# Attention with exchanged halves for the odd heads: products of both column halves beside each other, scores in quarters of the array

## The chip, the cores and the metric

The kernel runs on one core of a Trainium2 chip, as one program. The metric is the device time of one execution in microseconds; a kernel's time is the median of its runs. The core has five engines that matter here: PE (TensorE, matrix products, with a weight load recorded as PEld), DVE (VectorE), ACT (ScalarE), POOL (GpSimd) and SP (SyncE, which issues the DMAs). Each engine takes its instructions in order.

## The reference

Three parts follow one another, all in fp32. First a linear attention with a state, over 4 batches x 8 heads = 32 heads, 768 steps, 40 channels:

```python
for t in range(S):
    y[:, :, t] = np.einsum('bhd,bhde->bhe', rt, state)
    Sa = np.einsum('bhde,bhe->bhd', state, at)
    state_decay = state * wt[:, :, None, :] - np.einsum('bhd,bhe->bhde', Sa, bt)
    state = state_decay + np.einsum('bhd,bhe->bhde', vt, kt)
```

Then y, as 3072 tokens of 320 numbers, goes through a first expert, max(0.01 h, h) of h = x @ w_in (320 x 2048), times w_out, and through a second, sigmoid(x @ w_gate) * (x @ w_val) (1536 hidden), times w_out2.

## The kernel before, in words

**Chunks.** The 768 steps are cut into 12 chunks k of C = 64 steps; two make a block n (NB = 6), ci is the chunk in its block. The 32 heads are four groups q of eight. A group's eight heads are pairs: i = 0..3 counts pairs, h = 0, 1 the even and the odd head of a pair. Head h lies on partitions 64h to 64h+39 (D = 40 channels, the rest zeros).

**Preparation of a group (n, q).** `load` (L116) brings w, a and kb. In a the two heads of a pair stand block-diagonally, with zeros between them, so that one matmul of 128 x 128 gives both. `decays` (L138) runs cumulative products of w on DVE (L145, L151). `scale` (L156) multiplies a (L162) and kb (L165) by them, once per chunk; for block 0 part of this is on POOL, as the list `DVE0` says. `products` (L169) makes the scores sc of a against k and b, one matmul per chunk and pair (L177 to L179), one PSUM bank per chunk, and copies them out: ACT into Ld (L183) and Lo (L189), then the masked part against k into X, on DVE (L198), or on ACT and POOL for block 1 (L192, L195). `turned` (L202) transposes a (L209) and copies it into columns 64 to 103 of X (two copies a chunk, L214, one for each half of the partitions), then transposes kb (L217) into G (L220). `ranges` (L222) tests w.

**Solve.** `inverse` (L237) inverts the 32 x 32 triangles of all heads of a block, on POOL (on DVE for block 0). `solved` (L265) puts the inverse of 64 steps together with small products m (L279, L286) and multiplies it with X: the products qp (L294), copied to QT (L296).

**Recurrence.** `recur` (L315) takes one chunk of one group. It loads r into R (L326), v into W (L332) and, in `load_state` (L299), v transposed into FL (L303). The state is copied into W below v (L334). FL holds for each pair 64 columns of v transposed and 64 of the state transposed; the products fp of FL and R (L339) are masked into W (L341). The products pm of QT and W (L347) follow, one bank for each h, always on output partitions 64 to 127 (column half 64 to 128 of the array); ACT (L350) and DVE (L352) put them back into W. The products yp (L359, L362, L365) give the output y (L381) and the next state S (L369), which is transposed (L374) into FL of the next chunk (L376). In yp the heads alternate between output partitions 0 to 63 and 64 to 127.

**Order.** The order of the work is written out at the end of `attention` (L404 to L461): for each block n, groups in pairs; `together` (L395) runs the chunk of two groups in turns, four steps of the next block's inverse before each turn; the preparation of block n+2 stands around them. The program is built with a planner that simulates the engines and fixes each engine's order by it, so instructions of several stages mix. All DMAs are issued by SP, in order. The experts (class at L472, L598 on) come after; their weights are decoded by ACT, DVE and POOL when the attention ends.

**Layout.** `_layout` lays out the inputs on the host, outside the time.

Of the kernel before, what the change touches and what calls it, by code (L numbers as in the profile page):

```python
# [23 lines left out]
NQ, NX, NT = 10, 16, 2  # L24
HP = G // 2
C = 64
# [5 lines left out]
XF = 2 * C  # L32


def attention(ctx, tc, A, xT, bad, prods):
# [12 lines left out]
    masks = const.tile([128, 3, C], FP32, name="masks")  # L48
# [6 lines left out]
    TTx, G2x, Los, Gs, As, Rs, FLs, STs = [], [], [], [], [], [], [], []  # L55
    for i in range(2):
        Los.append(eb.tile([128, G, 32], FP32, bufs=1, name=f"Lo{i}"))
    for i in range(NX):
        Gs.append(two.tile([128, 8 * D + 24], FP32, bufs=1, name=f"G{i}"))
    for i in range(2):  # L60
        TTx.append(eb.tile([128, 8, 128], FP32, bufs=1, name=f"TTx{i}"))
        G2x.append(eb.tile([128, 8, 2, 32], FP32, bufs=1, name=f"G2x{i}"))
        As.append(ea.tile([128, 4, 2, 2, C], FP32, bufs=1, name=f"a{i}"))
# [8 lines left out]
    for i in range(6):  # L72
        STs.append(two.tile([128, 4, C], FP32, bufs=1, name=f"S{i}"))
        FLs.append(two.tile([128, 4, XF], FP32, bufs=1, name=f"FL{i}"))
# [13 lines left out]
    def zeros():  # L88

        for t in [t[:, 8 * D:] for t in Gs] + TTx + G2x + Rs + STs + [t[:, :, C:XF] for t in FLs] + Los[1:]:  # L90
            nc.gpsimd.memset(t, 0.0)
# [24 lines left out]
    def load(n, q):  # L116

        if q == 0:
            st["L", n] = (ea.tile([128, G, 32], FP32, tag="Ld", bufs=1, name="Ld"),
                          Los[n % 2])  # L120
        load_w(n, q)
        if n == 0 and q > 1:
            a = eb.tile([128, 4, 2, 2, C], FP32, tag="TTc", bufs=NT, name="a")
# [12 lines left out]
        st["in", n, q] = a, kb  # L136
# [31 lines left out]

    def products(n, q):  # L169


        a, kb = st["in", n, q]
        Ld, Lo = st["L", n]
        for ci in range(2):
            g0 = 8 * q + 4 * ci
            sc = bank(n, "sc")
            for i in range(4):  # L177
                nc.tensor.matmul(  # L178
                    out=sc[:, i].rearrange("p a s -> p (a s)"), lhsT=a[:, i, ci].rearrange("p a s -> p (a s)"),  # L179
                    rhs=kb[:, i, ci].rearrange("p a s -> p (a s)"), start=True, stop=True)  # L180
            for r in range(4):
                x, c0 = slice(32 * r, 32 * r + 32), 32 * (r % 2)
                nc.scalar.copy(out=Ld[x, g0:g0 + 4], in_=sc[x, :, 1, c0:c0 + 32])  # L183
# [3 lines left out]
            for r in (1, 3):  # L187
                x = slice(32 * r, 32 * r + 32)
                st["Lo", n, q] = nc.scalar.copy(out=Lo[x, g0:g0 + 4], in_=sc[x, :, 1, 0:32])  # L189
            X = eb.tile([128, 4, X1], FP32, tag="X", bufs=NX, name="X")  # L190
            if n == 1:
                nc.scalar.copy(out=X[:, :, 0:C], in_=sc[:, :, 0])  # L192
                for half in range(2):
                    x = X[64 * half:64 * half + 64, :, 0:C]
                    nc.gpsimd.affine_select(out=x, in_=x, pattern=[[0, 4], [-1, C]], base=0, channel_multiplier=1,  # L195
                                            compare_op=ALU.is_gt, fill=0.0)
            else:
                nc.vector.tensor_tensor(out=X[:, :, 0:C], in0=sc[:, :, 0], in1=bc(masks[:, 0], 4), op=ALU.mult)  # L198
            st["X", n, q, ci] = X
            st["G", n, q, ci] = Gs[(8 * n + 2 * q + ci) % NX]  # L200

    def turned(n, q):  # L202

        a, kb = st["in", n, q]
        for ci in range(2):
            X, g = st["X", n, q, ci], st["G", n, q, ci]
            tr = bank(n, "tr")
# [57 lines left out]
    def solved(n, q):  # L265
# [21 lines left out]
        for half in range(2):  # L287
            x = slice(64 * half, 64 * half + 32)
            nc.scalar.copy(out=tt[x, :, 64 * half + 32:64 * half + 64], in_=m2[0:32, :, half])
        for ci in range(2):  # L290
            X = st.pop(("X", n, q, ci))
# [4 lines left out]
            nc.scalar.copy(out=qt[0:X1].rearrange("p i h s -> p i (h s)"), in_=qp[0:X1])  # L296
            st["QT", n, q, ci] = qt

    def load_state(k, q):  # L299
# [3 lines left out]
        nc.sync.dma_start(out=FL[:, :, 0:C], in_=A["vT"][:, k, q])  # L303
# [8 lines left out]
    def by8(x):  # L312
        return x.rearrange("p e (u x) -> p e u x", x=8)

    def recur(n, q, ci):  # L315
# [12 lines left out]
        W = two.tile([128, X1 // 8, 8, 8], FP32, tag="W", bufs=3, name="W")  # L328
        we = W.rearrange("p u e x -> p e u x")
        Wv, Wf = we[:, :, 0:D // 8], we[:, :, D // 8:]  # L330
# [12 lines left out]
        cols, u0 = slice(0 if more else D, X1), 0 if more else D // 8  # L343
        for h in range(2):
            pm, e = bank2(n, "pm", [128, 4, 128]), slice(4 * h, 4 * h + 4)
            for i in range(4):
                nc.tensor.matmul(out=pm[C:2 * C, i, cols], lhsT=QT[0:X1, i, h], rhs=W[0:X1, u0:, 4 * h + i],  # L347
                                 start=True, stop=True)
            if more:
                st["Hs", n, q, ci] = nc.scalar.activation(out=Wv[C:2 * C, e], in_=by8(pm[C:2 * C, :, 0:D]),  # L350
                                                          func=AF.Copy, scale=-1.0)
            nc.vector.tensor_tensor(out=Wf[C:2 * C, e], in0=by8(pm[C:2 * C, :, D:X1]),  # L352
                                    in1=by8(bc(masks[C:2 * C, 2], 4)), op=ALU.mult)
# [3 lines left out]
        for j in range(2):  # L357
            for h in range(2):
                nc.tensor.matmul(out=yp[64 * h:64 * h + 64, 2 * j:2 * j + 2, D:X1], lhsT=FL[:, 2 * h + j, C:XF],  # L359
# [3 lines left out]
        for h, i, e in heads:  # L363
            g0 = D * (2 * i + h)
            nc.tensor.matmul(out=yp[64 * h:64 * h + 64, i, cols], lhsT=Gt[:, g0:g0 + 64], rhs=W[:, u0:, e],  # L365
                             start=False, stop=i == 3)
        if more:
# [8 lines left out]
            nc.scalar.copy(out=FL1[:, :, C:X1].rearrange("p (h j) d -> p j h d", h=2),  # L376
                           in_=st_.rearrange("p j (h d) -> p j h d", h=2)[:, :, :, 0:D])
# [443 lines left out]
def _layout(inputs):  # L821
# [16 lines left out]
    A["a"] = heads(a).reshape(2, D, NB, 2, 4, 4, C).transpose(0, 1, 2, 4, 5, 3, 6).reshape(2, D, NB, 4, 8, C)  # L838
    pairs = (2, 6, 4, 0, 3, 1, 5)
    A["r"] = r.reshape(B, 2, 2, 2, NC, C, D).transpose(pairs).reshape(2, D, NC, 4, 4, C)  # L840
    A["kb"] = np.stack([em(k), em(b)], 2).reshape(128, 4, 4, 2, NB, 2, C).transpose(0, 4, 1, 2, 5, 3, 6)
    vT = np.zeros((2, 64, NC, 4, 4, C), f)
    vT[:, :D] = v.reshape(B, 2, 2, 2, NC, C, D).transpose(pairs).reshape(2, D, NC, 4, 4, C)
    A["vT"] = vT.reshape(128, NC, 4, 4, C)
    A["v"] = v.reshape(B, 4, 2, NC, C, D // 8, 8).transpose(4, 3, 0, 5, 2, 1, 6).reshape(C, NC, 4, D // 8, 8, 8)
# [6 lines left out]
    m = np.zeros((128, 3, C), f)  # L852
    m[:, 0] = np.tile(low, (2, 1))
    m[:C, 1] = low.T
    m[C:X1, 1] = 1
    m[C:, 2] = -low.T
# [29 lines left out]
```

## Time and profile before

| | us |
|---|---|
| median of 3 runs (1284.63 to 1288.41) | 1285.53 |
| the profiled execution: its own time | 1287.13 |
| its span, first to last instruction | 1285.4 |
| PE busy in the span | 1173.8 |
| DVE, ACT, POOL busy | 749.9, 620.5, 328.3 |

Granted TensorE clock, mean over the span: 0.968 of full speed. The attention ends with the last y at 523 us; the experts take the rest.

How to read it: a row of the groups gives line, engine, operation, output<-inputs by the names in the program, shapes, count, then the busy time in us, the mean of one in ns, and the idle time of the engine just before such instructions with what ended it. A chain row is a piece of the path that ended last. Ends of matmuls are modelled, so two matmuls are compared by their starts; a few records of matmuls can be missing. Every fp32 matmul is recorded as two.

### The profile page before, as it was taken

What the parts mean: (1) busy time and instruction counts of PE and PEld (TensorE: products, weight loads), DVE (VectorE), ACT (ScalarE), POOL (GpSimd) and SP (SyncE); (2) the same over time, 40 slices, a digit from 0 to 9 for tenths busy, and PEclk for the clock granted to TensorE, in tenths of its full rate; (3) what the DMA queues carried; (4) which work ended last, traced back from release to release, by engine and by line L of the source; (5) the groups of instructions that cost most, each with busy time, mean ns of one, the idle gap of its engine ahead of it and who ended that gap; (6) DMA issues with size and microseconds to landing.
All of it is one profiled execution on the core that took longest, in us unless ns stands there. A gap on an engine that the chain in (4) does not pass through costs nothing.

```text
span 1285.4 us, 21419 instructions
## 1 busy us (share of the span) xinstructions
PE 1173.8 (91%) x7954; PEld 1006.9 (78%) x7954; DVE 749.9 (58%) x1455; ACT 620.5 (48%) x1510; POOL 328.3 (26%) x498
## 2 busy tenths in 40 slices
PE   4629988999889998899999999998999999999997
PEld 4528777888778887678778888887888888888886
DVE  9993766656663434899985444489972323222222
ACT  4737746667556453567664433356552323222221
POOL 9338373561726300244420000022320000000000
PEclk8769989999899999999999999999999999999999
DMA  6413224333231222433441010025320100000000
GB/s 192 126 44 88 76 64 106 108 85 83 57 84 48 66 67 68 120 101 103 117 121 40 21 46 26 21 81 151 105 80 1 46 1 21 1 21 1 21 1 24
DMA packets 105394, 84.54 MB, mean 66 GB/s; under 512 B 46656, under 2 KB 90432, under 8 KB 105280
## 3 DMA queue, kind: packets, MB, share of 16 engines
q1 hardware_dynamic: 105280, 83.07, 23.3%
q8 instruction: 65, 1.06, 0.3%
q14 instruction: 49, 0.40, 0.1%
HBM read 71.25 MB, written 11.80 MB: 65 GB/s over the span
## 4 chain that ended last, share of the span: by engine, by line
PE 66%; DVE 17%; ACT 8%; issue 4%; DMA 4%; POOL 1%; SPq 0%; DVEq 0%; ACTq 0%; POOLq 0%
PE h L579 18%; PE o L579 9%; PE o L595 9%; PE pm L347 5%; PE o L689 3%; PE o L690 3%; PE o L691 3%; PE qp L294 3%; ACT Ld L183 2%; PE fp L339 2%; DVE c L145 2%; PE yp L365 2%; DVE a L162 2%; PE m L279 1%; PE sc L178 1%
## 5 line engine op out<-in xcount | busy, mean ns | idle before, releaser
L579 PE MATMUL h<-xh,up 128*128 128x512 f32 x624 | 201.2, 394 | 8.5 <-DVE g L587 7.6
L579 PE MATMUL h<-xl,up 128*128 128x512 f32 x624 | 194.6, 392 | 0.0
L569 ACT CAST gh<-g 128x512 fp32r<-128x512 f32 x168 | 104.0, 620 | 176.8 <-DVE g L702 118.3
L570 DVE TENSOR_TENSOR gl<-g,gh 128x512 fp32r<-128x512 f32 x168 | 122.5, 730 | 72.3 <-ACT gh L569 72.2
L702 DVE TENSOR_TENSOR g<-o,t 128x512 f32<-128x512 f32 x72 | 49.6, 690 | 190.6 <-PE o L579 190.2
L579 PEld LDWEIGHTS h<-xh,up 128*128 128x128 f32 x624 | 116.7, 188 | 36.0 <-DVE g L587 10.3
L579 PEld LDWEIGHTS h<-xl,up 128*128 128x128 f32 x624 | 117.5, 189 | 22.8
L595 PE MATMUL o<-gh,down 128*128 128x512 f32 x450 | 132.0, 390 | 1.0 <-ACT gh L569 1.0
L698 ACT ACTIVATE t<-h 128x512 f32<-128x512 f32 x72 | 42.9, 596 | 126.5 <-PE h L579 126.4
L595 PEld LDWEIGHTS o<-gh,down 128*128 128x128 f32 x450 | 84.5, 188 | 19.4 <-ACT gh L569 1.8
L587 DVE TENSOR_TENSOR g<-h,t 128x512 f32<-128x512 f32 x96 | 65.8, 686 | 55.6 <-ACT t L586 55.2
L250 POOL TENSOR_TENSOR tmp<-T 128x30 f32<-128x30 f32 (+9 forms) x150 | 86.7, 578 | 42.1 <-DVE T L243 28.8
L511 POOL TENSOR_TENSOR down<-f,e 128x256 fp32r<-128x256 f32 (+2 forms) x41 | 39.7, 983 | 225.9 <-PE o L595 171.4
L347 PE MATMUL pm<-W,QT 104*64 104x104 f32 (+1 forms) x768 | 80.9, 261 | 14.9 <-DVE W L341 14.2
L595 PE MATMUL o<-gl,down 128*128 128x512 f32 x270 | 90.4, 389 | 0.0
L579 PE MATMUL o<-xh,up 128*128 128x512 f32 x288 | 89.2, 390 | 0.5 <-POOL up L511 0.5
L255 POOL TENSOR_TENSOR T<-T,tmp 128x30 f32<-128x30 f32 (+9 forms) x150 | 86.4, 576 | 11.1
L579 PE MATMUL o<-xl,up 128*128 128x512 f32 x288 | 88.5, 389 | 0.0
L347 PEld LDWEIGHTS pm<-W,QT 104*64 104x64 f32 x768 | 71.1, 142 | 20.7 <-DVE W L341 15.3
L586 ACT ACTIVATE t<-h 128x512 f32<-128x512 f32 x96 | 56.7, 592 | 61.1 <-PE h L579 61.0
L689 PE MATMUL o<-down,gh 128*128 128x320 f32 x264 | 80.1, 309 | 0.4 <-ACT gh L569 0.4
L690 PE MATMUL o<-down,gh 128*128 128x320 f32 x264 | 80.3, 308 | 0.0
(267 smaller groups left out, 2337.4 us busy)
## 6 DMA issues: line engine op xcount, KB each, us to landing
kb<-in_kb SPq DMA_DIRECT2D x24, 512.0 KB
rd<-in_w_out SPq DMA_DIRECT2D x28, 320.0 KB
w<-in_w SPq DMA_DIRECT2D x24, 260.5 KB
FL<-in_vT SPq DMA_DIRECT2D x48, 128.0 KB
ru<-in_w_in SPq DMA_DIRECT2D x16, 384.0 KB
ru<-in_w_gate SPq DMA_DIRECT2D x12, 384.0 KB
ru<-in_w_val SPq DMA_DIRECT2D x12, 384.0 KB
a<-in_a SPq DMA_DIRECT2D x48, 80.0 KB
```

The lines of the kernel that those rows point to most:

```text
L250: eng.tensor_tensor(out=tv, in0=T[:, i0:i1, j:j + 1].to_broadcast([128, i1 - i0, j]), in1=T[:, j:j + 1, 0:j].to_broadcast([128, i1 - i0, j ...
L255: steps.append(eng.tensor_tensor(out=T[:, i0:i1, 0:j], in0=T[:, i0:i1, 0:j], in1=tv, op=ALU.add))
L347: nc.tensor.matmul(out=pm[C:2 * C, i, cols], lhsT=QT[0:X1, i, h], rhs=W[0:X1, u0:, 4 * h + i], start=True, stop=True)
L569: copy = self.nc.scalar.copy(out=gh, in_=g)
L570: self.last = copy.ins, (engine or self.nc.vector).tensor_tensor(out=gl, in0=g, in1=gh, op=ALU.subtract).ins
L579: self.nc.tensor.matmul(out=ps, lhsT=l, rhs=r, start=(i == 0), stop=(i == len(ops) - 1))
L586: self.nc.scalar.activation(out=t, in_=h, func=AF.Copy, scale=0.01)
L587: self.nc.vector.tensor_tensor(out=g, in0=h, in1=t, op=ALU.max)
L595: self.nc.tensor.matmul(out=acc, lhsT=l, rhs=r, start=first and i == 0, stop=last and i == len(ops) - 1)
L689: nc.tensor.matmul(out=o, lhsT=gj, rhs=w[:, 0], start=s, stop=False)
L690: nc.tensor.matmul(out=o, lhsT=gj, rhs=w[:, 1], start=False, stop=False)
L702: nc.vector.tensor_tensor(out=g, in0=pv, in1=s, op=ALU.mult)
```

## The change

The zeros between the heads of a pair go, and the odd heads' operands stand in exchanged halves of the partitions.

- a is loaded without zeros, [2 chunks, 4 pairs, 64] instead of [4, 2, 2, 64], and scaled by one operation. The scores of a chunk for two pairs are four small matmuls over 40 rows and 64 columns, one for each quarter of the array (h chooses the rows, f the columns), where they were two over the whole array; each h has its own bank, instead of each chunk. For odd heads the host exchanges k and b in kb.
- One transpose turns two pairs of a at once, so four per group and block instead of eight, and one copy instead of four puts them into X.
- X is [128, 4, 4, 64], eight fixed buffers: for even heads scores then a, for odd heads a then scores. The gaps are zeroed once on POOL. The weights of qp are 128 columns instead of 104.
- FL holds, for a pair of heads, v, state, state, v. The weights of fp are 128 columns instead of 104. W is split by h; v is loaded by two DMAs instead of one, and vT too. The mask on fp is two operations of 256 columns instead of one of 512.
- pm of even heads goes to partitions 64 to 127, of odd heads to 0 to 63, in turns, in one bank.

The core of the diff (declarations, zeroing, the masks' layout on the host and renamed views are left out):

```diff
@@ load, scale
-            nc.sync.dma_start(out=a.rearrange("p i c h s -> p (i c) h s")[64 * h:64 * h + D, :, h], in_=A["a"][h, :, n, q])
+            nc.sync.dma_start(out=a[64 * h:64 * h + D], in_=A["a"][h, :, n, q])
...
+        eng = nc.vector if n or (q, 0) in DVE0 else nc.gpsimd
+        eng.tensor_tensor(out=a, in0=a, in1=c.rearrange("p i c s -> p c i s")[:, :, :, 0:C], op=ALU.mult)
         for ci in range(2):
             eng = nc.vector if n or (q, ci) in DVE0 else nc.gpsimd
-            eng.tensor_tensor(
-                out=a[:, :, ci], in0=a[:, :, ci],
-                in1=c[:, :, ci:ci + 1, 0:C].to_broadcast([128, 4, 2, C]), op=ALU.mult)
@@ products
-            for i in range(4):
-                nc.tensor.matmul(
-                    out=sc[:, i].rearrange("p a s -> p (a s)"), lhsT=a[:, i, ci].rearrange("p a s -> p (a s)"),
-                    rhs=kb[:, i, ci].rearrange("p a s -> p (a s)"), start=True, stop=True)
+            for j in range(2):
+                for h, f in ((0, 0), (1, 1), (0, 1), (1, 0)):
+                    i, d = 2 * j + f, slice(64 * h, 64 * h + D)
+                    nc.tensor.matmul(
+                        out=scs[h][64 * f:64 * f + 64, 2 * ci + j].rearrange("p a s -> p (a s)"),
+                        lhsT=a[d, ci, i], rhs=kb[d, i, ci].rearrange("p a s -> p (a s)"), start=True, stop=True)
@@ turned
-            for i in range(4):
+            for j in range(2):
                 nc.tensor.transpose(
-                    out=tr[:, i].rearrange("p a s -> p (a s)")[:, 0:X1],
-                    in_=a[0:X1, i, ci].rearrange("p a s -> p (a s)"), identity=ident[0:X1, 0:X1])
-            for half in range(2):
-                x = slice(64 * half, 64 * half + 64)
-                nc.scalar.copy(out=X[x, :, C:X1], in_=tr[x, :, half, 0:D])
+                    out=tr[:, 2 * ci + j, 0:X1], in_=a[0:X1, ci, 2 * j:2 * j + 2].rearrange("p f s -> p (f s)"),
+                    identity=ident[0:X1, 0:X1])
+        nc.scalar.copy(out=st["X", n, q][:, :, 1:3, 0:D],
+                       in_=tr.rearrange("p a (h d) -> p a h d", h=2)[:, :, :, 0:D])
@@ solved
-            for i in range(4):
-                nc.tensor.matmul(out=qp[0:X1, i], lhsT=X[:, i], rhs=tt[:, 4 * ci + i], start=True, stop=True)
+            for j in range(2):
+                for h in range(2):
+                    nc.tensor.matmul(out=qp[:, 2 * j + h], lhsT=X[:, 2 * ci + j, 2 * h:2 * h + 2].rearrange("p a s -> p (a s)"),
+                                     rhs=tt[:, 4 * h + 2 * ci + j], start=True, stop=True)
@@ load_state
-        nc.sync.dma_start(out=FL[:, :, 0:C], in_=A["vT"][:, k, q])
+        for h in range(2):
+            nc.sync.dma_start(out=FL[:, :, 3 * h], in_=A["vT"][:, k, q, h])
@@ recur
+        rows, ns = (slice(0, X1), slice(0, 128)), (D, C)
+        top, own = (slice(0, C), slice(C, 2 * C)), (slice(C, 2 * C), slice(0, C))
         if more:
-            nc.sync.dma_start(out=W[0:C, 0:D // 8], in_=A["v"][:, k, q])
             for h in range(2):
-                (nc.scalar.copy if h else nc.vector.tensor_copy)(out=Wv[C:X1, 4 * h:4 * h + 4],
-                               in_=by8(ST[64 * h:64 * h + D, :, 0:D]))
+                nc.sync.dma_start(out=W[top[h], h, 0:D // 8], in_=A["v"][h, :, k, q])
+            for h in range(2):
+                (nc.scalar.copy if h else nc.vector.tensor_copy)(
+                    out=we[own[h].start:own[h].start + ns[h], h, :, 0:D // 8], in_=by8(ST[64 * h:64 * h + ns[h], :, 0:D]))
...
-                nc.tensor.matmul(out=fp[0:X1, 4 * h + 2 * j:4 * h + 2 * j + 2], lhsT=FL[:, 2 * h + j, 0:X1],
+                nc.tensor.matmul(out=fp[:, 4 * h + 2 * j:4 * h + 2 * j + 2], lhsT=both(FL[:, j, 2 * h:2 * h + 2]),
                                  rhs=R[:, :, 2 * h + j], start=True, stop=True)
-        nc.vector.tensor_tensor(out=Wf[0:X1], in0=by8(fp[0:X1]), in1=by8(bc(masks[0:X1, 1], 8)), op=ALU.mult)
+        for h in range(2):
+            nc.vector.tensor_tensor(out=we[:, h, :, D // 8:], in0=by8(fp[:, 4 * h:4 * h + 4]),
+                                    in1=by8(bc(masks[:, 1 + h], 4)), op=ALU.mult)
         yield
         cols, u0 = slice(0 if more else D, X1), 0 if more else D // 8
+        pm = bank2(n, "pm", [128, 4, 128])
+        for h, i, e in heads:
+            nc.tensor.matmul(out=pm[own[h], i, cols], lhsT=QT[rows[h], 2 * (i // 2) + h, i % 2], rhs=W[rows[h], h, u0:, i],
+                             start=True, stop=True)
         for h in range(2):
-            pm, e = bank2(n, "pm", [128, 4, 128]), slice(4 * h, 4 * h + 4)
-            for i in range(4):
-                nc.tensor.matmul(out=pm[C:2 * C, i, cols], lhsT=QT[0:X1, i, h], rhs=W[0:X1, u0:, 4 * h + i],
-                                 start=True, stop=True)
```

## Rows read from the trace of the kernel before

**Rows 1.** The page, part 1: each engine's busy time over the whole span.

```profile
PE 1173.8 (91%) x7954; PEld 1006.9 (78%) x7954; DVE 749.9 (58%) x1455; ACT 620.5 (48%) x1510; POOL 328.3 (26%) x498
```

**Rows 2.** The view by stretches: the attention's first stretch and its main loop.

```profile
core 0: us, PE busy (x) PEld busy (x) DVE busy (x) ACT busy (x) POOL busy (x), PEclk, DMA share, GB/s
0.00:93.00 93.00, 39.70 (x256) 36.11 (x256) 87.08 (x217) 50.48 (x174) 50.17 (x82) 0.77 0.45 125
93.00:512.00 419.00, 381.71 (x4056) 335.83 (x4057) 236.51 (x445) 246.03 (x738) 186.75 (x332) 0.97 0.29 75
```

**Rows 3.** The chain of waits, first stretch (first row), then main loop (start us, us, what).

```profile
by line: ACT Ld L183 12.4%; DVE c L145 9.2%; issue 7.3%; DVE tmp L250 7.2%; DVE T L255 7.1%; DVE rc L151 6.5%; ACT Lo L189 6.4%; DVE a L162 5.3%; PE sc L178 4.4%; ACT X L214 4.0%; ACT w L226 3.3%; DMA w<-in_w 3.1%; ACT G L220 3.1%; ACT X L1
...
by line: PE pm L347 15.1%; PE qp L294 9.0%; PE fp L339 6.6%; PE yp L365 6.2%; issue 5.3%; PE m L279 4.4%; ACT Ld L183 4.4%; DVE c L145 4.3%; DVE a L162 4.2%; PE yp L359 3.8%; PE sc L178 3.3%; PE m L286 3.2%; PE yp L362 2.9%; ACT Lo L189 2.5
...
411.03 1.75 PE fp L339 x16
412.78 1.76 PE qp L294 x16
```

**Rows 4.** Groups by line, main loop: the products pm (both widths).

```profile
L347 PE MATMUL pm<-W,QT 104*64 104x104 f32 (+1 forms) x736 | 78.6, 262 | 14.8 <-DVE W L341 14.0 <-issue 0.7
```

**Rows 5.** The timeline of PE in the main loop (start us, us, engine, line, operation).

```profile
351.26 0.52 PE L209 MATMUL tr<-ident,a 104*128 104x104 f32 x4
351.62 0.52 PE L217 MATMUL tr<-ident,kb 104*128 104x104 f32 x4
...
354.29 2.05 PE L178 MATMUL sc<-kb,a 128*128 128x128 f32 x16
356.18 0.52 PE L209 MATMUL tr<-ident,a 104*128 104x104 f32 x4
...
361.60 1.64 PE L347 MATMUL pm<-W,QT 104*64 104x104 f32 x16
363.17 1.08 PE L279 MATMUL m<-TTx,Lo 128*32 128x64 f32 x16
364.18 1.37 PE L347 MATMUL pm<-W,QT 104*64 104x104 f32 x13
365.30 0.32 PE L359 MATMUL yp<-R,FL 128*64 128x128 f32 x1
...
366.66 0.93 PE L365 MATMUL yp<-W,G 128*64 128x104 f32 x16
367.42 0.61 PE L359 MATMUL yp<-R,FL 128*64 128x128 f32 x8
...
368.43 0.30 PE L286 MATMUL m<-G2x,Ta 128*32 128x64 f32 x2
368.65 0.39 PE L365 MATMUL yp<-W,G 128*64 128x104 f32 x2
368.98 0.30 PE L286 MATMUL m<-G2x,Ta 128*32 128x64 f32 x2
```

**Rows 6.** Groups by line, main loop, DVE and then ACT.

```profile
L352 DVE TENSOR_TENSOR W<-pm,masks 64x256 f32<-64x256 f32 x92 | 38.1, 427 | 53.2 <-ACT W L350 52.7
L341 DVE TENSOR_TENSOR W<-fp,masks 104x512 f32<-104x512 f32 x47 | 32.0, 682 | 47.3 <-PE fp L339 47.3
...
L162 DVE TENSOR_TENSOR a<-a,c 128x512 f32<-128x512 f32 x28 | 20.6, 768 | 0.0
...
L214 ACT COPY X<-tr 64x160 f32<-64x160 f32 x64 | 18.4, 287 | 0.9
...
L220 ACT COPY G<-tr 128x320 f32<-128x320 f32 x32 | 13.7, 427 | 24.5 <-PE yp L365 24.2
```

**Rows 7.** SP's queue: its longest wait in the attention, then two lines' issues.

```profile
SPq L326 <- PE yp L359: 168.8, 24, 15.2
...
L303 SPq DMA_DIRECT2D FL<-in_vT x48: 378/401/1070, 13.3 to 495.9; - x48
...
L332 SPq DMA_DIRECT2D W<-in_v x44: 471/472/1203, 18.9 to 500.0; - x44
```

More of the change, by code (lines that the diff above doesn't have):

```diff
@@ L47, in attention @@
     ident = const.tile([128, 128], FP32, name="ident")
-    masks = const.tile([128, 3, C], FP32, name="masks")
+    masks = const.tile([128, 4, C], FP32, name="masks")
     mask32 = const.tile([128, 32], FP32, name="mask32")
@@ L54, in attention @@
     endv = ends.rearrange("p (a s) -> p a s", s=C + 1)
-    TTx, G2x, Los, Gs, As, Rs, FLs, STs = [], [], [], [], [], [], [], []
+    TTx, G2x, Los, Gs, As, Rs, FLs, STs, Xs = [], [], [], [], [], [], [], [], []
     for i in range(2):
         Los.append(eb.tile([128, G, 32], FP32, bufs=1, name=f"Lo{i}"))
-    for i in range(NX):
+    for i in range(NG):
         Gs.append(two.tile([128, 8 * D + 24], FP32, bufs=1, name=f"G{i}"))
@@ L62, in attention @@
         G2x.append(eb.tile([128, 8, 2, 32], FP32, bufs=1, name=f"G2x{i}"))
-        As.append(ea.tile([128, 4, 2, 2, C], FP32, bufs=1, name=f"a{i}"))
+        As.append(ea.tile([128, 2, 4, C], FP32, bufs=1, name=f"a{i}"))
+    for i in range(NX):
+        Xs.append(eb.tile([128, 4, 4, C], FP32, bufs=1, name=f"X{i}"))
     for i in range(3):
@@ L73, in attention @@
         STs.append(two.tile([128, 4, C], FP32, bufs=1, name=f"S{i}"))
-        FLs.append(two.tile([128, 4, XF], FP32, bufs=1, name=f"FL{i}"))
+        FLs.append(two.tile([128, 2, 4, C], FP32, bufs=1, name=f"FL{i}"))
     nc.gpsimd.memset(As[0], 0.0)
@@ L88, in zeros @@
     def zeros():
-        for t in [t[:, 8 * D:] for t in Gs] + TTx + G2x + Rs + STs + [t[:, :, C:XF] for t in FLs] + Los[1:]:
+        for t in ([t[:, 8 * D:] for t in Gs] + TTx + G2x + Rs + STs + [t[:, :, 1:3] for t in FLs] + Los[1:]
+                  + [t[:, :, 1:3, D:C] for t in Xs]):
             nc.gpsimd.memset(t, 0.0)
@@ L122, in load @@
         if n == 0 and q > 1:
-            a = eb.tile([128, 4, 2, 2, C], FP32, tag="TTc", bufs=NT, name="a")
+            a = eb.tile([128, 2, 4, C], FP32, tag="TTc", bufs=NT, name="a",
+                        padded_shape=[128, 4, 4, C])
             nc.gpsimd.memset(a, 0.0)
@@ L173, in products @@
         Ld, Lo = st["L", n]
+        X = st["X", n, q] = Xs[(4 * n + q) % NX]
+        scs = [bank(n, "sc") for h in range(2)]
         for ci in range(2):
-            g0 = 8 * q + 4 * ci
-            sc = bank(n, "sc")
-            for i in range(4):
-                nc.tensor.matmul(
-                    out=sc[:, i].rearrange("p a s -> p (a s)"), lhsT=a[:, i, ci].rearrange("p a s -> p (a s)"),
-                    rhs=kb[:, i, ci].rearrange("p a s -> p (a s)"), start=True, stop=True)
+            for j in range(2):
[5 more added lines that the diff above has]
+        for h in range(2):
+            sc, g0 = scs[h], 8 * q + 4 * h
             for r in range(4):
                 x, c0 = slice(32 * r, 32 * r + 32), 32 * (r % 2)
-                nc.scalar.copy(out=Ld[x, g0:g0 + 4], in_=sc[x, :, 1, c0:c0 + 32])
+                nc.scalar.copy(out=Ld[x, g0:g0 + 4], in_=sc[x, :, 1 - h, c0:c0 + 32])
             x = Ld[:, g0:g0 + 4]
@@ L188, in products @@
                 x = slice(32 * r, 32 * r + 32)
-                st["Lo", n, q] = nc.scalar.copy(out=Lo[x, g0:g0 + 4], in_=sc[x, :, 1, 0:32])
-            X = eb.tile([128, 4, X1], FP32, tag="X", bufs=NX, name="X")
+                st["Lo", n, q] = nc.scalar.copy(out=Lo[x, g0:g0 + 4], in_=sc[x, :, 1 - h, 0:32])
             if n == 1:
-                nc.scalar.copy(out=X[:, :, 0:C], in_=sc[:, :, 0])
+                nc.scalar.copy(out=X[:, :, 3 * h], in_=sc[:, :, h])
                 for half in range(2):
-                    x = X[64 * half:64 * half + 64, :, 0:C]
+                    x = X[64 * half:64 * half + 64, :, 3 * h]
                     nc.gpsimd.affine_select(out=x, in_=x, pattern=[[0, 4], [-1, C]], base=0, channel_multiplier=1,
@@ L313, in by8, with both @@
         return x.rearrange("p e (u x) -> p e u x", x=8)
+    def both(x):
+        return x.rearrange("p a s -> p (a s)")
     def recur(n, q, ci):
@@ L358, in recur @@
             for h in range(2):
-                nc.tensor.matmul(out=yp[64 * h:64 * h + 64, 2 * j:2 * j + 2, D:X1], lhsT=FL[:, 2 * h + j, C:XF],
+                nc.tensor.matmul(out=yp[64 * h:64 * h + 64, 2 * j:2 * j + 2, D:X1], lhsT=FL[:, j, 1 + h],
                                  rhs=R[:, :, 2 * h + j], start=j == 0, stop=False)
@@ L364, in recur @@
             g0 = D * (2 * i + h)
-            nc.tensor.matmul(out=yp[64 * h:64 * h + 64, i, cols], lhsT=Gt[:, g0:g0 + 64], rhs=W[:, u0:, e],
+            nc.tensor.matmul(out=yp[64 * h:64 * h + 64, i, cols], lhsT=Gt[:, g0:g0 + 64], rhs=W[:, h, u0:, i],
                              start=False, stop=i == 3)
@@ L851, in _layout @@
     low = (i[None, :] < i[:, None]).astype(f)
-    m = np.zeros((128, 3, C), f)
+    m = np.zeros((128, 4, C), f)
     m[:, 0] = np.tile(low, (2, 1))
-    m[:C, 1] = low.T
-    m[C:X1, 1] = 1
-    m[C:, 2] = -low.T
+    m[:C, 1] = m[C:, 2] = low.T
+    m[C:X1, 1] = m[:D, 2] = 1
+    m[:, 3] = -np.tile(low.T, (2, 1))
     A["masks"] = m
```

41 lines of the change are left out of this document (20 added, 21 removed).

## The prediction

> **What bounds the kernel now.** I read the page's engine shares first: PE is busy 1173.8 of 1285.4 us, the others under 60% [rows 1]. An average over two different halves says little, so next come the stretches. From about 512 us on the experts run, which the change doesn't touch; their weights are decoded after the attention, so I let that half shift as a whole. The attention has two stretches [rows 2]: 0 to 93 us, where DVE is busy 87.08 of 93 us and PE only 39.70, and 93 to 512 us, the main loop, where PE is busy 381.71 of 419 us (91%), DVE 236.51, ACT 246.03, POOL 186.75. The reader is to see that the same edit is worth DVE time in the first stretch and PE time in the second.
>
> Busy is not yet path, so third is the chain of waits by line [rows 3]. In the main loop its largest item is pm, 15.1% of 419 us, 63 us; qp has 9.0% (38 us), fp 6.6%, sc 3.3% (14 us), and the scaling of a on DVE 4.2% (17.6 us). In the first stretch the scaling has 5.3% of 93 us (4.9), sc 4.4% (4.1), the copies into X 4.0% (3.7). PE's idle time in front of pm is 14.8 us in all [rows 4]: little is lost waiting, the array itself is slow.
>
> Fourth, the PE timeline, where spacings are read from start to start [rows 5]. Every fp32 matmul is two records. A pm block of 16 records, all on columns 64 to 128, begins at 361.60 and the next tile at 363.17: 1.57 us. A yp block of 16 records of the same 104 columns, which alternate between the two column halves, takes 366.66 to 367.42: 0.76 us, 48 ns each. That pair of rows is the core of my argument: two halves of the array run beside each other.
>
> **Part by part, main loop.**
>
> Change of tile shape. In the timeline two m records (which pass in 363.17 to 364.18, 16 in 1.01 us, 63 ns each) need 368.43 to 368.65 when yp follows, 0.22 instead of 0.13, and two yp records need 368.65 to 368.98, 0.33 instead of 0.10 [rows 5]. So a change costs 0.09 to 0.23 us; I take 0.15. The scores now have a shape of their own, which adds about one change to a block: 16 blocks lie in the loop, 2.4 us; the ends are 0 and two changes of 0.23, 7.4 us. The Trainium skill, "TensorEngine Tiling (Array Packing)", section Tiling Modes, says that changing the tiling mode drains the engine. The trace agrees, at 0.09 to 0.23 us; were there no drain, the sum would be 2.4 us better.
>
> pm, both column halves. A block of 16 without its change of shape takes 1.57 - 0.15 = 1.42 us, 89 ns a record; at yp's spacing 0.76, so 0.66 saved. That holds for the first chunk of a pair. The second chunk's last three pm records already run beside yp (yp starts at 365.30, before pm has ended [rows 5]), 0.27 us that was hidden before, so 0.39 there. 22 x 0.66 + 22 x 0.39 = 23.1, and the four chunks with only 64 columns give about 0.3 each: 24.3 us of PE.
>
> Scores. A block takes 354.29 to 356.18, 1.89 us, 118 ns a record [rows 5]. After: 32 records of a quarter of the array. No row shows two row halves beside each other. From below: all four quarters at once, 118/4 = 29.5 ns, 0.94 us. From above for a working overlap: only column halves, 59 ns, 1.89 us, no gain; no overlap at all is a rival below. I take 34 ns, as the halving of columns gave 48/89 and twice that factor is 0.29: 32 x 0.034 = 1.09, with the change 1.24 us, 0.65 saved, 16 blocks: 10.4 us (ends +2.4 and -15).
>
> Transposes of a: 8 records become 4; at (351.62 - 351.26)/4 = 90 ns [rows 5] this is 0.36 x 16 = 5.8 us.
>
> fp and qp load 128 columns of weights where they loaded 104: 16 records take 1.75 us, 109 ns, now [rows 3], and sc with 128 columns takes 118 [rows 5]. The ends are nothing (a transpose, with 128 columns too, goes at 90 ns) and 9 ns; half of it on some 760 records costs 3.4 us.
>
> PE in all: -24.3 - 10.4 - 5.8 + 3.4 = -37 us of 382.
>
> DVE: the scaling of a, 28 ops of 0.768 in the loop [rows 6], covers 1,024 slots of which half are zeros; 14 ops remain, -10.3 us. The mask on fp is cut into two of 256: 2 x 0.427 by the row of that width in place of 0.682, +0.17 x 47 = +8 us. ACT: 64 copies of 0.287 into X become 16 of 0.427 (the row of 128x320), -11.6 us [rows 6]. Neither engine binds in the loop.
>
> Issues. v and vT are each loaded by two DMAs for one: 44 + 48 more issues on SP, at 0.40 to 0.47 us some 40 us of that queue. SP waits 168.8 us in front of L326 alone [rows 7], so I cost them at nothing; behind them in the queue stand R, a, kb and w of the next chunks, and if the slack is gone R and then fp come about 0.9 us later per chunk. The swap of kb's halves is made on the host. The added memsets of X's gaps are on POOL, busy 50.17 of the first 93 us [rows 2], while its scaling of a falls from four ops to one. Both are costed at nothing; if POOL is late there, zeros arrive late for the first solve.
>
> **What of it lies on the path.** I weigh each term by the share of its busy time that the chain holds. pm: 63 of 78.6 us [rows 3, 4], 0.8, so -19.4. sc: 14 us of the chain against 16 blocks of 1.89, 0.45, so -4.7. Transposes, not among the chain's named lines, 0.3: -1.7. fp and qp 0.65: +2.2. The scaling of a is halved on the chain: -8.8. The second mask op I charge at a third: +3. Loop: -29.4 us. First stretch: scaling -2.5, scores -1.3 (a third), copies into X -2.3: -6. Together -35 us. The profiled execution took 1287.1 us (span 1285.4 and 1.7 around it), 1.6 over the median of the runs, 1285.5. So 1287.1 - 35 = 1252, and 1251 as a median. The order on each engine is planned again for the new instructions, which can move single waits in either direction; I have no row for that, and keep some 12 us on both sides.
>
> What is late next: with a pm block of 0.8 us the products end sooner than ACT and DVE can take them out. DVE's op on pm already idles 52.7 us behind ACT's op on the same block [rows 6], and both heads now share one bank, so four reads of 0.3 and 0.43 us follow each other.
>
> **Rivals.**
>
> A, the reads take over. PE gets free time but the round from fp over mask, pm, its reads, yp and the state is no shorter: pm's 0.66 us returns as a wait before yp. For it: the 52.7 us. Against: ACT and DVE are under 60% busy, and other chunks' work fills PE. A third of the loop's 29 us passes, and the 6 us of the first stretch: 1287 - 16 - 2 = 1269. The same page of the Trainium skill, section Performance Considerations, says that tiling speeds TensorE and not the emptying of PSUM; by this rule it would be this case, and the trace's 91% of PE against 56 to 59% of the readers speaks rather against it. 22%.
>
> B, slower: the quarters of the scores pass one after another. Then 32 x 0.118 + 0.15 = 3.93 us a block, +2.04 x 16 = +32.6 us on an engine that binds, and +4.4 on the first chain; the other terms of the loop give -24.7 and of the first stretch -4.8. Sum +7.5: 1293 as a median. It decides where a record takes over about 105 ns. For it: no row shows row halves apart. Against: column halves do run beside each other. 7%.
>
> C, more than forecast: all 37 us of PE come through and the waits in front of PE shrink as ACT and DVE are lighter: -37 - 9 + 3 - 6 and some 3 of waits, about -52: 1234. For it: PE's 91%. Against: a chain that is cut lets the next one through. 12%.
>
> That the edit does nothing at all (the scores in pairs, pm without overlap since both halves read different rows) leaves transposes, scaling and X: about -10, 1275. 3%.
>
> **How the numbers follow.** 56% for the forecast, with 1240 to 1263 as its own range, 22 A, 12 C, 7 B, 3 for the last. A range of 1230 to 1275 holds all but B and the outer part of C. About 0.3%, 3.9 us, is what a measurement of this kernel can tell from no change. Faster: forecast, A, C and most of the last, 0.90; slower: B, 0.07, less where it ends near zero; same 0.03.
>
> **What would show it right or wrong.** Right: pm blocks of 16 in 0.76 to 0.85 us; 32 score records in 1.0 to 1.3 us; four transposes of a per block; PE busy in the loop down by some 35 us while the last y of the attention comes 30 to 40 us sooner; the experts' half unchanged in length. A shows as PE idle in front of yp and pm, released by DVE W or ACT W, grown by over 15 us. B shows as score spacings near 118 ns. The forecast is wrong too if PE's granted clock in the loop falls below the 0.97 of before [rows 2], as a less busy PE had low spells in the first stretch (0.77): each point of it costs about 4 us of loop.

## The result: 1273.9 us, ratio 0.987, and the profile after

| | before | after |
|---|---|---|
| median, us (runs of after 1268.36 to 1276.08) | 1285.53 | 1273.88 |
| ratio to before | | 0.9872 [0.9838, 0.9905] |
| the profiled execution, its span | 1287.13, 1285.4 | 1274.33, 1272.6 |
| granted clock over the span | 0.968 | 0.948 |

The forecast was 1251. The time lies in the range of 1230 to 1275, but 12 us came by the medians, some 16 by the ratio, where 35 were named. The ratio is that of the record, for which the kernel before had four runs (1284.63 to 1295.62, median 1286.97); the two medians of the table alone give 0.991. The page's first part and the view by stretches, of the kernel after:

```profile
PE 1155.9 (91%) x8242; PEld 977.1 (77%) x8242; DVE 738.3 (58%) x1482; ACT 603.2 (47%) x1438; POOL 316.4 (25%) x503
```

```profile
0.00:93.00 93.00, 44.65 (x437) 38.35 (x438) 83.76 (x211) 50.42 (x165) 46.00 (x100) 0.74 0.42 125
93.00:512.00 419.00, 368.78 (x4277) 311.58 (x4276) 241.92 (x512) 236.04 (x693) 183.15 (x326) 0.91 0.31 82
```

Against [rows 2] PE is busy 13 us less in the same 419 us, though more of the attention now fits into them, and its granted clock is 0.91 where it was 0.97: more stretches at 1.2 GHz in place of 2.4. The first stretch got 8.6 us shorter (the first transpose into TTc starts at 81.4 for 90.0 us). From there to the end of the last y, 429.0 us pass for 433.7. The experts' half did not move (762.3 for 761.7).

For each profile I cut this loop, first TTc to last y, into three parts that add up to it: PE's idle time; what the half clock costs (half of the time in which PE is busy at the granted 1.2 GHz); and the rest, PE's work as it would take at full clock. All are summed from PE's records and the granted clock, in us:

| kernel | loop | PE's work at full clock | cost of the clock | PE idle |
|---|---|---|---|---|
| before | 433.7 | 378.6 | 12.9 | 42.1 |
| after | 429.0 | 339.8 | 35.2 | 54.0 |
| after, a second profile | 426.7 | 341.1 | 28.0 | 57.6 |
| after_floor (same loop, below) | 430.0 | 344.3 | 27.0 | 58.7 |

So PE's work fell by 34 to 39 us, near the forecast (37). The clock took 14 to 22 of it and waits 12 to 17. The plan moves PE's work too: the control below (turned_order), with equal products in another order, has 332.8, which is 7 to 12 less. The products ran as argued; PE's timeline after (start us, us, line, count, idle before):

```profile
135.00 2.53 PE L300 MATMUL qp<-TTx,X 128*128 128x128 f32 x16 [2.10 <-issue]
137.45 3.69 PE L183 MATMUL sc<-kb,a 40*64 40x128 f32 x64
141.08 1.65 PE L362 MATMUL pm<-W,QT 104*64 104x104 f32 x16
...
157.00 1.95 PE L300 MATMUL qp<-TTx,X 128*128 128x128 f32 x16
158.78 1.06 PE L353 MATMUL fp<-R,FL 128*128 128x128 f32 x8
159.77 0.94 PE L362 MATMUL pm<-W,QT 104*64 104x104 f32 x16
160.64 1.08 PE L284 MATMUL m<-TTx,Lo 128*32 128x64 f32 x16
```

```profile
289.57 1.98 PE L183 MATMUL sc<-kb,a 40*64 40x128 f32 x64
291.48 0.93 PE L362 MATMUL pm<-W,QT 104*64 104x104 f32 x16
```

A pm block takes 159.77 to 160.64, 0.87 us for 1.57 [rows 5]; 64 score records take 289.57 to 291.48, 30 ns each, a quarter of the 118 before. The same 64 records behind a wait of 2.10 us, at 137.45, take 3.63 us: that is the half clock, which the trace has from 136.3 to 143.2 us. The waits that count, in the loop of after (engine, line, releaser: us, times, longest):

```profile
DVE W L368 <- ACT W L366: 35.8, 49, 3.6
...
ACT W L366 <- DVE W L368: 31.9, 33, 3.1
...
PE yp L381 <- DVE W L368: 15.3, 8, 7.1
...
PE pm L362 <- DVE W L356: 5.8, 4, 2.2
```

Before, PE waited 14.0 us in front of pm [rows 4]. That wait fell to 5.8, and one before yp, for the state's products read back into W, took its place. The longest, 7.1 us, shows what stood in the way; ACT first, then PE and DVE:

```profile
291.94 1.06 ACT L190 COPY Ld<-sc 32x128 f32<-32x128 f32 x4
293.03 0.53 ACT L196 COPY Lo<-sc 32x128 f32<-32x128 f32 x2
...
298.78 0.53 ACT L196 COPY Lo<-sc 32x128 f32<-32x128 f32 x2
299.33 0.72 ACT L231 ACTIVATE w<-w,half 128x512 f32<-128x512 f32 x1
299.96 0.19 ACT L231 ACTIVATION_READ_ACCUMULATOR w<-w,half 128x1 f32 x1
300.17 0.30 ACT L366 ACTIVATE W<-pm 64x160 f32<-64x160 f32 x1
```

```profile
294.55 0.54 PE L378 MATMUL yp<-S,ident 128*128 128x160 f32 x2
302.21 0.61 PE L381 MATMUL yp<-W,G 128*64 128x104 f32 x2 [7.13 <-DVE W L368]
```

```profile
299.68 2.02 DVE L248 STREAM_TRANSPOSE T<-Ld 128x1024 f32<-128x1024 f32 x1
301.73 0.43 DVE L368 TENSOR_TENSOR W<-pm,masks 64x256 f32<-64x256 f32 x1
```

The pm block at 291.48 is done by 292.4. But ACT has the score reads of two groups and two tests of w planned in one piece, 291.94 to 300.15, and reads pm only behind them; DVE then puts the transpose of Ld first. PE, with the scores done early, has nothing left to do.

At this place of the loop the kernel before has the same reads in two pieces, with a read of pm between them; ACT there:

```profile
305.77 1.06 ACT L183 COPY Ld<-sc 32x128 f32<-32x128 f32 x4
...
308.48 0.53 ACT L189 COPY Lo<-sc 32x128 f32<-32x128 f32 x2
309.03 0.30 ACT L350 ACTIVATE W<-pm 64x160 f32<-64x160 f32 x1
309.35 0.72 ACT L226 ACTIVATE w<-w,half 128x512 f32<-128x512 f32 x1
```

The longest run of score reads and tests of w in the loop of before is 4.9 us. Every kernel with the change has four runs of 8.2 us, except where the spreading below parts them. So the long run came with the new plan; which part of the change made the planner put it there, no run separates.

### The profile page after: what moved, and what is told of

The parts are those of the page before. It is cut to its first block, busy times and chain, and to the rows that moved or that the text cites. A ratio compares the mean times of both kernels' runs of the same rounds, so it can differ in the third digit from the quotient of the medians.

```text
span 1272.6 us, 22040 instructions
## 1 busy us (share of the span) xinstructions
PE 1155.9 (91%) x8242; PEld 977.1 (77%) x8242; DVE 738.3 (58%) x1482; ACT 603.2 (47%) x1438; POOL 316.4 (25%) x503
## 4 chain that ended last, share of the span: by engine, by line
PE 62%; DVE 18%; ACT 7%; DMA 5%; issue 5%; POOL 4%; SPq 0%; DVEq 0%; ACTq 0%; POOLq 0%
PE h L594 18%; PE o L594 9%; PE o L610 8%; PE o L704 3%; PE o L705 3%; PE o L706 3%; PE qp L300 3%; PE yp L381 3%; PE fp L353 3%; PE pm L362 2%; DMA ru<-in_w_val 2%; ACT Ld L190 2%; PE m L284 2%; DVE z L513 2%; PE m L291 2%
## 5 line engine op out<-in xcount | busy, mean ns | idle before, releaser
L610 PE MATMUL o<-gh,down 128*128 128x512 f32 x450 | 134.6, 393 | 0.2 <-ACT gh L584 0.2
L526 POOL TENSOR_TENSOR down<-f,e 128x256 fp32r<-128x256 f32 (+2 forms) x41 | 43.0, 1063 | 234.1 <-PE o L610 172.4
L602 DVE TENSOR_TENSOR g<-h,t 128x512 f32<-128x512 f32 x96 | 65.8, 686 | 57.9 <-ACT t L601 57.6
L255 POOL TENSOR_TENSOR tmp<-T 128x30 f32<-128x30 f32 (+9 forms) x150 | 82.1, 547 | 40.3 <-DVE T L248 27.2
L381 PE MATMUL yp<-W,G 128*64 128x104 f32 (+1 forms) x768 | 62.3, 279 | 15.4 <-DVE W L368 15.3
L526 POOL TENSOR_TENSOR up<-f,e 128x384 fp32r<-128x384 f32 x38 | 44.1, 1160 | 110.8 <-DVE e L520 100.4
```

What stands on the lines that cost most here:

```text
L255: eng.tensor_tensor(out=tv, in0=T[:, i0:i1, j:j + 1].to_broadcast([128, i1 - i0, j]), in1=T[:, j:j + 1, 0:j].to_broadcast([128, i1 - i0, j ...
L526: nc.gpsimd.tensor_tensor(out=out, in0=f[:, c0:c1], in1=ef[:, c0:c1], op=ALU.mult)
L602: self.nc.vector.tensor_tensor(out=g, in0=h, in1=t, op=ALU.max)
L610: self.nc.tensor.matmul(out=acc, lhsT=l, rhs=r, start=first and i == 0, stop=last and i == len(ops) - 1)
```

## The experiments

Each ratio is against runs of the kernel before on the same chip. "Loop" is that of the table, and the loops are what I compare: the ratios also hold the first stretch, which is about 8 us longer in some executions of one and the same kernel (last section).

**Undo the two column halves of pm alone** (pm_apart) **and the mixing of the quarters** (sc_pairs).

```diff
-        for h, i, e in heads:
+        for h, i, e in sorted(heads):
```
```diff
-            for j in range(2):
-                for h, f in ((0, 0), (1, 1), (0, 1), (1, 0)):
+            for h, j in ((0, 0), (0, 1), (1, 0), (1, 1)):
+                for f in range(2):
```

> The same kernel after the change, but the eight pm products of a chunk are issued all four of one head parity first, then the four of the other, so that the column halves no longer pass in turns. A pm block of 16 records goes from 0.87 us (start to start, with its change of shape) to about 1.5 us. Theory 1 (PE's work is no longer what the loop waits for: the planned order on ACT and DVE puts other work ahead of pm's reads, PE waits, its granted clock falls, and the saved time is lost there): pm's 0.6 us a block fills waits; half-clock time in the loop shrinks from 75 us and the time stays within 5 us of the changed kernel, 1269 to 1279. Rival 2 (PE still binds, and the saving of pm did arrive but was eaten by unrelated slower pieces): 40 blocks x 0.6 x 0.8 = +19 us, 1290 to 1296.

> The same kernel after the change, but the score products of a group go in the order even heads first, then odd heads, so that only two column halves pass beside each other and the row halves one after another. A block of 32 records goes from 0.95 us (30 ns a record) to about 1.9 us. Theory 1: within 5 us of the changed kernel; ACT can begin on the first bank half a block earlier, so the waits of PE do not grow. Rival 2 (PE binds): 16 blocks x 0.95 = +15 us in the loop, less what was off the chain, so +7 to +15 us.

pm_apart: 0.9924 [0.9897, 0.9951], PE's work 355.6, 11 to 16 more than after, and loop 437.7, 8 to 11 more, which lies between the two theories. A pm block there, from PE's timeline:

```profile
104.48 1.34 PE L362 MATMUL pm<-W,QT 104*64 104x104 f32 x16
105.75 0.88 PE L183 MATMUL sc<-kb,a 40*64 40x128 f32 x22
```

79 ns a record, so the alternation is what makes pm short. The wait before yp is still 14.2 us, 6.8 at its longest, so it does not need the quick pm products. sc_pairs did not do what it was made for: 0.9942 [0.9925, 0.9958], but the blocks of scores at full clock still took 31 ns a record and PE's work was 343.4. This order does not spoil the overlap, and the run says nothing on what the quarters are worth.

**Move score reads apart** (spread): the preparation of group 3 goes between the two chunks, so ACT's run is cut in two, as it was before the change.

```diff
-                for p in (2, 3):
-                    early(n + 2, p)
+                early(n + 2, 2)
             together((n, q, 0), (n, q + 1, 0))
+            if more and q == 2:
+                early(n + 2, 3)
```

> The same kernel after the change, but in the second half of each block n the preparation of group 3 of block n+2 is written after the first pair of chunks, and no longer directly behind that of group 2, so that the four score banks of the two groups need not be read by ACT in one run ahead of pm's reads. Theory 1: the waits of PE of 1.5 to 7 us at the four places where DVE turns Ld into T shrink to about 1 us each (some 15 us in all), the half-clock stretches behind them (about 3.4 to 6.8 us each) go, and the time falls by 8 to 20 us, to 1254 to 1266. Rival 2 (other work sets the round; the waits at these places only show where the slack lies): the same waits appear elsewhere and the time stays within 4 us of the changed kernel.

0.9726 [0.9699, 0.9754]; loop 416.5, with PE's work 343.4, clock 24.0, idle 49.1. In the loop's waits:

```profile
PE pm L362 <- DVE W L356: 8.8, 5, 2.1
...
PE yp L381 <- DVE W L368: 2.8, 7, 0.6
```

The wait before yp falls from 15.3 to 2.8 us, the loop by 12.5 (against the other two profiles of after 10.2 and 13.5). Of that, 5 to 10 us are idle time, since other waits grew a little, and 3 to 11 the clock. The cause of that wait is shown by its removal; what the removal is worth depends on the rest of the plan, as the pairs below show.

**Fill PE's waits** (dummies): six products with no use ahead of yp, for the first chunk of groups 2 and 3 in the first four blocks.

```diff
+        if n < 4 and q > 1 and ci == 0:
+            for _ in range(6):
+                nc.tensor.matmul(out=yp.rearrange("p a s -> p (a s)")[:, 0:256], lhsT=ident,
+                                 rhs=masks.rearrange("p a s -> p (a s)"), start=True, stop=True)
```

> The same kernel after the change, with six additional products of the identity and the masks (128 x 256, fp32, 0.43 us each at full clock, 2.6 us together) into the yp bank ahead of yp, for the first chunk of groups 2 and 3 in blocks 0 to 3: eight times, 21 us of PE in all. Their results are overwritten by yp. They stand where PE waited for pm's reads in the changed kernel. Theory 1, with the clock as the larger part of the loss: the granted clock no longer falls behind these places, the loop's mean clock rises from 0.91 to 0.94 or more, and the time stays or falls by up to 8 us in spite of 21 us more work. If the clock is a small part of the loss, or the products do not hold it: the clock stays at 0.91 and the time grows by 0 to 12 us. Rival 2 (PE binds): +15 to +20 us.

1.0055 [1.0025, 1.0086], loop 453.3: PE's work 365.1, clock 28.2, idle 60.0. The wait before yp fell to 6.4 us, but one of 8.2 us came up in front of a transpose of kb; the clock stayed low and the idle time did not fall, so this settles nothing on the clock. The loop grew by 23 to 27 us for 21 to 25 of added work. That is nearest to the theory by which PE still binds (15 to 20), and above it: work put into PE at this place passes whole into the loop.

**The kernel after again, one bank for each head of pm** (two_banks, `pms = [bank2(n, "pm", [128, 4, 128]) for h in range(2)]`), **both edits** (spread_two), **and the spreading alone on the kernel before** (before_spread).

> The changed kernel itself, once more, on the chip of the three kernels that run beside it, so that they can be compared directly. All theories: a ratio of 0.984 to 0.991 to the kernel before, as first measured; waits and half-clock time in the loop as in its first profile (50 us and 81 us, each within a quarter).

> The changed kernel with one PSUM bank for pm of the even and one for pm of the odd heads, as before the change, and the column halves still in turns. Takes away the wait of ACT's second read of pm on DVE's first read (31.9 us in 33 waits in the changed kernel, none before), behind which ACT's other copies for PE stand. Theory 1: this is part of why PE waits, so PE's idle time in the loop falls by 5 to 15 us and the time by 4 to 15 us. Rival 2 (the one long run of score reads is the whole of it): the waits at the four turns of Ld into T stay, the time stays within 4 us.

> Both: the preparation of group 3 behind the first pair of chunks, and two banks for pm. If the two waits are separate causes, the gains add: 4 to 12 us below the kernel with the spread preparation alone, a ratio of 0.962 to 0.970 to the kernel before. If the planner only places the same waits elsewhere, the ratio stays at 0.970 to 0.976.

> The kernel before the change with the preparation of group 3 behind the first pair of chunks, nothing else. Theory 1 (the spreading pays because the change made PE outrun the readers): before the change PE waited only 0.7 to 1.0 us at each of the four turns of Ld into T, so the ratio to the kernel before is 0.995 to 1.005. Rival 3 (the order gains by itself, whatever the products cost, and has nothing to do with the change): the same 12 to 19 us as on the changed kernel, a ratio of 0.985 to 0.990.

after_again 0.9924 [0.9898, 0.995]; two_banks 0.9971 [0.9937, 1.0006]; spread_two 0.9891 [0.9838, 0.9944]; before_spread 1.0036 [1.001, 1.0062]. Separate banks did not pay: loops 431.8 and 423.9, so the shared bank is not the bound. Spreading does not speed the kernel before (loop 439.5, for 433.7), whose reads were in two pieces already.

**A comparison with a tile instead of a constant** (after_floor, spread_floor), for a hold in the first stretch that is told below; **the spreading with pm's halves apart** (spread_apart); **and a control** (turned_order), which only turns the order of the pm products round, with `heads[::-1]`.

```diff
-        nc.vector.tensor_scalar(out=last, in0=c.rearrange("p a b s -> p (a b) s")[:, :, C:C + 1],
-                                scalar1=1e-30, scalar2=None, op0=ALU.max)
+        nc.vector.tensor_tensor(out=last, in0=c.rearrange("p a b s -> p (a b) s")[:, :, C:C + 1],
+                                in1=tiny.unsqueeze(1).to_broadcast([128, 8, 1]), op=ALU.max)
```

> The changed kernel with one DVE operation in another form: the floor of 1e-30 under the cumulative products (128 x 8) is a maximum of two tensors, and no longer of a tensor and a constant. In half of the profiles after the change this operation in the first stretch takes 9.39 us where it takes 0.63 in the others and 0.16 to 0.2 later, and it ends together with POOL's run of zeroing memsets; the two forms differ in nothing else that the plan sees. If the constant form is what waits for POOL: the operation stays under 1 us in the profile, and no execution has the late first stretch, so the median falls by 3 to 8 us against the changed kernel (ratio 0.983 to 0.988), with a narrower spread of its runs. If any DVE operation there waits: the 9 us stay in about half of the runs and the median stays within 3 us.

> The preparation of group 3 behind the first pair of chunks, and the floor as a maximum of two tensors: both edits that helped or should help. Theory 1 and the hold by POOL together: 1253 to 1262 us, a ratio of 0.968 to 0.974, every run in the lower group. If the first result of the spread order was luck of its four runs: 0.976 to 0.982.

> The spread order with the pm products of even heads first and then of odd heads, not in turns. On the changed kernel the same edit cost 0.2 to 0.5%. Theory 1: where PE waits less, its work is worth more, so without the turns the time grows by 8 to 18 us over the spread order (44 blocks of 0.6 us, a third to two thirds on the path), a ratio of 0.979 to 0.987. Rival 2 (the halves of pm are off the path whatever the order): within 4 us of the spread order, 0.970 to 0.976.

> A control: the changed kernel with pm's eight products in the reverse order, still in turns of the two halves. No engine gets more or less work; only the plan of the engines' orders comes out otherwise (about a thousand of PE's rows move in it). It shows how far a new plan alone moves the time: both theories expect at most 6 us either way, a ratio of 0.985 to 0.995. A larger move would mean that differences of this size between the other kernels can be the plan's alone.

after_floor 0.9873 [0.9837, 0.991]; spread_floor 0.9756 [0.9726, 0.9787], 1257.87 us, loop 415.7, the fastest median of all here together with spread (1260.44); spread_apart 0.9986 [0.9956, 1.0016]; turned_order 0.9957 [0.9934, 0.998]. With spread_floor the gain of spreading came a second time (loop 14.3 us under after_floor). With separate banks it is 7.9 us, and with pm's halves apart only 1.4 (spread_apart 436.3, pm_apart 437.7): there the wait before yp fell too, from 14.2 to 4.3 us, but other waits and 8 us more of PE's work took the gain. The ACT timeline of spread_floor shows the cut:

```profile
293.47 0.53 ACT L198 COPY Lo<-sc 32x128 f32<-32x128 f32 x2
294.02 0.72 ACT L233 ACTIVATE w<-w,half 128x512 f32<-128x512 f32 x1
294.65 0.19 ACT L233 ACTIVATION_READ_ACCUMULATOR w<-w,half 128x1 f32 x1
294.86 0.30 ACT L368 ACTIVATE W<-pm 64x160 f32<-64x160 f32 x1
295.66 0.30 ACT L368 ACTIVATE W<-pm 64x160 f32<-64x160 f32 x1
296.52 1.06 ACT L192 COPY Ld<-sc 32x128 f32<-32x128 f32 x4 [0.39 <-PE sc L185]
```

spread_apart loses 19.8 us of loop against spread, where pm_apart lost 8 to 11 against after: pm's halves are worth about twice as much once the long run is gone. The control's loop is 432.4, 2 to 6 us over after, with one order of equal products turned. That is what a new plan does by itself, and differences of this size (two_banks, sc_pairs) are not read as effects.

**Take DVE work out of both kernels** (after_light, before_light): the scaling of kb is left out for blocks 2 to 5.

```diff
-            st["kb", n, q, ci] = eng.tensor_tensor(
+            st["kb", n, q, ci] = n < 2 and eng.tensor_tensor(
```

> The kernel after, without the scaling of kb (L167) for blocks 2 to 5; kb stays unscaled there, so part of the computation is left out. In the loop this takes about 28 operations off DVE, some 23 us of its busy time, and nothing off PE. If the queues of DVE and ACT set the loop after the change, it gets 10 to 25 us shorter, and PE's idle time falls with it. If PE at its half clock sets it, DVE's lighter queue is worth 0 to 5 us, unless the half-clock time falls too.

> The kernel before with the same scaling of kb (L165) left out for blocks 2 to 5. PE was the bound there by the prediction, so a lighter DVE is worth little: 0 to 8 us. If it is worth as much as in the kernel after, DVE's queue bound both kernels alike, and the change did not move the bound.

after_light 0.9886 [0.9821, 0.9951], before_light 0.9937 [0.9905, 0.9969]. The stretch 93 to 512 us of after_light, and its wait before yp:

```profile
93.00:512.00 419.00, 362.17 (x4262) 304.95 (x4260) 219.15 (x481) 234.18 (x687) 176.93 (x322) 0.92 0.31 81
```

```profile
PE yp L381 <- DVE W L368: 18.1, 4, 7.1
```

DVE has 23 us less to do, yet the loop is 430.4 us, no shorter, with 60.6 idle and 29.0 for the clock. The theory that DVE's load took over falls. ACT's long run is left by this edit, and so is the wait of 7.1 us. The kernel before got 6 us out of its loop (427.4), about the size of the control. In before_light the planner put ACT's reads into four runs of 7.3 us, and PE still does not wait before yp: with the slow products of before, PE has work left for as long as ACT reads.

## Why the prediction went wrong, point by point

- **PE's terms**: right. pm blocks 0.87 us (0.76 to 0.85 named); pm's busy time in the loop 53.7 for 78.6 us [rows 4], 24.9 less where 24.3 stood. Scores 30 ns a record for 34. Four transposes of a for a group and block. In all 34 to 39 us for 37.
- **DVE and ACT terms**: right, but for the second mask operation, whose busy time rose by 3.5 us where 8 stood. The loop's groups after, a line each of DVE and ACT, against 20.6, 32.0 and 18.4 us [rows 6]:

```profile
L356 DVE TENSOR_TENSOR W<-fp,masks 128x256 f32<-128x256 f32 x96 | 35.5, 412 | 54.8 <-PE fp L353 54.1
...
L164 DVE TENSOR_TENSOR a<-a,c 128x512 f32<-128x512 f32 x14 | 9.6, 682 | 0.0
```

```profile
L216 ACT COPY X<-tr 128x320 f32<-128x320 f32 x16 | 6.8, 423 | 1.2 <-PE tr L213 1.0
```

- **The first stretch**: -6 was forecast, and -8.6 came: 2.9 ahead of T, which starts at 34.3 for 37.2, and 5.7 from there to TTc (47.1 for 52.8 us). In the second profile, with the hold told in the last section, TTc comes at 89.6, as late as before.
- **Issues on SP at nothing**: held. The wait in front of r's load (L326 before, L337 after) fell from 168.8 [rows 7] to 60.7 us, so the slack was used but was there; PE waited 2.7 us for R in the loop.
- **The step that failed** is "What of it lies on the path": each term weighed by its share of the chain of before, -29.4 us in the loop, with the waits and the clock of before left as they were. A chain's share tells what lay on the path while the plan was as it was. The loop fell by 4 to 7 us, because waits grew by 12 to 17 us and the clock cost 14 to 22 more. The allowance of 12 us for the new plan was too small for that. Rival A had the place right ("pm's 0.66 us returns as a wait before yp", 1269), at 22%. Its cause was only partly right: not pm's saved time that returns (pm_apart has the wait without it), but ACT's run of score reads in front of pm's reads, which the kernel before had in two pieces. I had looked at the ACT and DVE shares of 56 to 59% as evidence against A. A share says nothing of 8 us in one piece. The Trainium skill, "TensorEngine Tiling (Array Packing)", section Performance Considerations, warns that the emptying of PSUM may become the bottleneck; the trace agrees in that the reads of PSUM hold PE up for 7.13 us, with ACT busy under half of the span.
- **The clock** stood under what would make the forecast wrong, at 4 us for each point. It fell by 6 points, 24 us by that price, and the sum gives 14 to 22. It was put at nothing in the sum, though the first stretch showed a less busy PE at 0.77 [rows 2].
- **How the two share the loss** stays open. Three profiles of the same loop have 35.2, 28.0 and 27.0 us of clock cost and 429.0, 426.7 and 430.0 us of loop: where the clock cost less, waits and PE's work took most of it back. So a loop without low spells would not simply be 28 us shorter. No run held the clock up with the order unchanged.
- **Rivals B and C**: the quarters run beside each other, so B is out; C's shrinking waits did not come.

## What to carry to other kernels

When an edit makes the busiest engine faster in a loop whose order is planned, compare the planned orders of before and after on the engines that read its results, and look for long runs of other work that were not there (here 8 us of score reads): there a gain can turn into a wait. Then move such runs apart. Cut the time into work at full clock, clock and idle before you judge an edit: a part can do all that it promised and show little in the total. Turn something of no consequence as a control, to learn what a new plan alone does (here 2 to 6 us).

## What was not expected of the hardware

**A small DVE operation held by POOL's zeroing.** In the second profile of the kernel after the maximum with a constant over 128x8 elements (L151) takes 9.39 us, and everything after it comes 8 us later (first TTc at 89.6 for 81.4). First DVE, then POOL:

```profile
19.48 9.39 DVE L151 TENSOR_SCALAR prods<-c 128x8 f32<-128x8 f32 x1
```

```profile
18.29 0.91 POOL L93 MEMSET G<- 128x24 f32 x16
...
27.20 1.65 POOL L93 MEMSET X<- 128x192 f32 x8
```

It ends with POOL's run of memsets, at 28.85 us. In the first profile of the same kernel it takes 0.63 us with the same memsets beside it:

```profile
19.17 0.63 DVE L151 TENSOR_SCALAR prods<-c 128x8 f32<-128x8 f32 x1
```

So it comes and goes from run to run. Even in the first profile a later one of the same line (at 27.16 us) takes 1.45 us and ends at 28.61, with the memsets. The profiles of pm_apart, sc_pairs, spread_two, spread_apart and turned_order have the long hold (9.39 to 9.41 us), and their first TTc starts at 89.3 to 89.9 us; those of spread, two_banks, dummies and after_light don't (78.9 to 80.6). before_light shows it too (7.72 us), so the change did not bring it; the eight memsets of X, costed at nothing, make it 1.65 us longer. With a tile in place of the constant (after_floor, spread_floor) it was 0.17 us, and the runs of after_floor lie within 1271.82 to 1274.19. Two kernels without a held operation do not show that the form is what matters, since other kernels escaped as well.

**The first stretch does not feel the clock.** after_floor had full clock up to 81 us and after 0.75, and their first TTc starts at 80.2 and 81.4. The view by stretches, after and then after_floor:

```profile
0.00:81.00 81.00, 36.78 (x352) 30.68 (x352) 77.76 (x207) 43.35 (x147) 41.27 (x87) 0.75 0.48 144
```

```profile
0.00:81.00 81.00, 37.78 (x352) 31.52 (x352) 77.69 (x210) 43.13 (x147) 41.90 (x87) 1.00 0.48 144
```

**Four quarters of the array run fully beside each other** at fp32: 30 ns a record where the whole array takes 118 [rows 5] and two column halves 48 to 54, with each row half in a bank of its own.
